# Copies of keys and queries in the token stage: one ScalarE instruction of 1280 columns, or two of 640 with a step between

## The chip, the cores and the metric

The kernel runs on one core of a Trainium2 chip. The metric is the device time of one execution in microseconds (us), as the median of several runs. Engines are called PE (TensorE, matrix products), PEld (its weight loads), DVE (VectorE), ACT (ScalarE), POOL (GpSimd) and SP (SyncE, which issues most DMAs).

## The reference

Agent attention over 4 batches of 10048 tokens with 128 channels and 49 agents, then a mixture of 16 experts (4 groups of 4) on its output, one expert per token:

```python
a2k = sm(agents, k)              # softmax over 10048 keys, 49 x 10048 per batch
agent_v = a2k @ v                # 49 x 128
q2a = sm(q, agents)              # 10048 x 49
x = (q2a @ agent_v).reshape(40192, 128)
g_idx = argmax(x @ w_group); e_idx = argmax(x[group g] @ w_expert[g])
out[token] = g_w * e_w * (relu(x @ w1[g, e]) @ w2[g, e])      # 128 -> 1024 -> 128
```

Here sm is a softmax of the scaled product, and g_w and e_w are the softmax weights of the chosen group and expert.

## The kernel before

Products run in 16-bit floats with a split: a float32 tile x is taken as an upper half xh = fp16(x) and a lower half xl = x - xh, and products are summed over the halves. So keys, queries, values and the hidden layer each need a copy to fp16, which ACT makes, and a subtraction for the lower half, which DVE or POOL makes.

The work has three stages. In the opening (to about 55 us) the first batch's keys, values and part of its queries are worked through, and its most used expert is chosen. The token stage (about 55 to 730 us) is a stream: for three batches in the order SEQ, 20 tiles of 512 tokens each, it computes the batch's main expert on every token. Each tile has 8 units. A unit is `first` (two PE products of 512 columns into a PSUM tile ph, of which there are three buffers; `evicted`: ACT writes hh = relu(ph) as fp16, DVE writes the lower half hl, and only then is ph free) and, eight units behind, `second` (three products into po). A last stage works the fourth batch, whose tokens have been sorted by expert.

Between the units of the token stage lies side work for the batches that come later in the stream: key scores, values, query scores, routing. It is written as Python generators, called lanes (`QUEUE`: q0 to q3 are queries, k1 to k3 keys and values, a0 to a3 what follows, p3 the sorting transfers). After each unit `advance` deals steps of lanes: the one that is furthest behind its due share goes first, as long as a budget of DVE and ACT time per unit (`RATE`, 900 and 1100 ns) is not used up. The time of an instruction is counted by `Counted`; for ACT it is 190 ns and 0.83 ns per column. A lane's progress is the sum of these, ACT's with weight 0.7 (`WL`), over a fixed total (`TOTALS`: 55.1e3 for a key lane, 26.2e3 for a query lane). A generator that yields an integer n isn't taken up again before n units have passed (`HOP` is 2); a bare yield lets others go on in the same unit. Where a tile of the stream needs something that isn't there, `own_tile` forces lanes on without regard to these.

`split_load` (from line 276) makes the halves of one chunk of keys or queries: 10 tiles of 128 tokens, 1280 columns (`CT * P`), the last one of a batch 1152 or 1088. It takes the loaded float32 tile xf, issues one ACT copy xh of all columns, yields HOP, and then issues POOL's subtractions for xl in pieces of 256 columns, five per full chunk. The scores of the chunk (`key_scores`, `query_scores`) come later in the lane and use xh and xl on PE: for each group of five tiles first the products with xh, then those with xl. The tiles xh and xl have three buffers each, shared with the values' halves. In the opening (`early` given, or `wide[0]` true) the same function works ahead of the stream; `wide[0]` becomes false where the token stage begins.

Each engine executes its instructions in the order of its own queue. On ACT the copies stand between the stream's evictions hh, on POOL the pieces of xl stand between the lower halves of the values (sl), of the softmax rows (rows) and sums (S). In the profile all PE, DVE and ACT instructions have line 140, that of the counting helper, so they are told apart by tile names; L304 is POOL's xl.

Of the kernel before, what the change touches and what calls it, by code (L numbers as in the profile page):

```python
# [13 lines left out]
AF = mybir.ActivationFunctionType  # L14
# [6 lines left out]
P = 128  # L21
# [34 lines left out]
HT = CT // 2  # L56
# [22 lines left out]
HOP = 2  # L79
# [68 lines left out]
def build(ctx, tc, qT, kT, v, agT, wr, w1, w2, cpk, out, cols):  # L148
# [5 lines left out]
    act = Counted(nc.scalar, work, 2, 190.0, 0.83)  # L154
# [19 lines left out]
    wide = [True]  # L174
# [17 lines left out]
    def load(kind, b, ci, xf=None):  # L192

        t0, t1 = chunks[ci]
        n = min(N, t1 * P) - t0 * P
        if xf is None:
            xf = stg.tile([P, CT * P], F32, name="xf", tag="xf")
        sync.dma_start(out=xf[:, 0:n], in_=(qT if kind == "q" else kT)[b][:, t0 * P:t0 * P + n])
        if kind == "q" and n < (t1 - t0) * P:
            vec.memset(xf[:, n:(t1 - t0) * P], 0.0)  # L200
        return xf
# [74 lines left out]
    def split_load(kind, b, ci, early=None):  # L276
        t0, t1 = chunks[ci]
        n = (t1 - t0) * P if kind == "q" else min(N, t1 * P) - t0 * P
        if (kind, b, ci) in halves:
            lane("q0")["done"] += halves.pop("work") if "work" in halves else 0.0  # L280
            yield HOP
            return halves.pop((kind, b, ci))
        xf = loaded.pop((kind, b, ci), None) if early is None else first_loads[kind, ci]
        if early is not None and kind == "k" and ci < NB:
            xh = wbuf[ci].bitcast(F16)[:, 2 * CT * P:3 * CT * P]
            xl = early.tile([P, CT * P], F16, name="xs", bufs=4)
        elif early is not None and kind == "k" and ci > len(chunks) - 3:
            xh, xl = [early.tile([P, CT * P], F16, name="xs", bufs=4) for _ in range(2)]
        else:
            if xf is None:  # L290
                xf = load(kind, b, ci)
            xh = wk.tile([P, CT * P], F16, name="xh", tag="xh")
            xl = wk.tile([P, CT * P], F16, name="xl", tag="xl")
        act.activation(xh[:, 0:n], xf[:, 0:n], AF.Copy)
        if early is None:
            yield HOP
        a = 0
        if early is not None and kind == "k":
            a = min(n, SHARED)
            vec.tensor_sub(out=xl[:, 0:a], in0=xf[:, 0:a], in1=xh[:, 0:a])  # L300
        if a < n:
            for a in range(a, n, GP):
                z = min(n, a + GP)
                pool.tensor_sub(out=xl[:, a:z], in0=xf[:, a:z], in1=xh[:, a:z])  # L304
        return xh, xl
# [49 lines left out]
    def key_load(b, ci, early=None):  # L355

        st = state[b]
        if ci == 0:
            st["S"] = rt.tile([P, NT, NA], F32, name="S", tag="S")
            st["most"] = rt.tile([P, CT, NA], F32, name="most", tag="most")  # L360
            st["part"] = []
        st["k", ci] = yield from split_load("k", b, ci, early)
        yield
# [427 lines left out]
    def query_load(b, ci, x, early):  # L791
        x["x"] = yield from split_load("q", b, ci, early)
        yield
# [549 lines left out]
    def split_ahead():  # L1343

        which = next(x for x in loaded if x[0] == "q")
        w = work.copy()
        g = split_load(*which)
        while True:
            try:
                next(g)  # L1350
            except StopIteration as x:
                halves[which] = x.value
                halves["work"] = halves.get("work", 0.0) + float(np.dot(work - w, WL))
                break
# [338 lines left out]
    def lane(name):  # L1693
        return next(y for y in lanes if y["name"] == name)
# [157 lines left out]
```

## Time and profile before

| | us |
|---|---|
| median of 3 runs | 914.24 (911.54 to 914.42) |
| profiled execution | 907.38 |
| its span, first to last instruction | 905.1 |
| PE busy in the span | 844.7 (93%) |
| DVE busy | 710.8 (79%) |
| ACT busy | 613.8 (68%) |
| POOL busy | 462.9 (51%) |
| mean granted TensorE clock | 0.982 |

Busy times are unions of instruction spans on one engine. PE is pipelined and the ends of its products are modelled, so a PE that is shown busy is not one at its peak. The profiled execution is one of many and lies below the three timed runs.

### The profile page before, as it was taken

What the parts mean: (1) busy time and instruction counts of PE and PEld (TensorE: products, weight loads), DVE (VectorE), ACT (ScalarE), POOL (GpSimd) and SP (SyncE); (2) the same over time, 40 slices, a digit from 0 to 9 for tenths busy, and PEclk for the clock granted to TensorE, in tenths of its full rate; (3) what the DMA queues carried; (4) which work ended last, traced back from release to release, by engine and by line L of the source; (5) the groups of instructions that cost most, each with busy time, mean ns of one, the idle gap of its engine ahead of it and who ended that gap; (6) DMA issues with size and microseconds to landing.
All of it is one profiled execution on the core that took longest, in us unless ns stands there. A gap on an engine that the chain in (4) does not pass through costs nothing.

```text
span 905.1 us, 22546 instructions
## 1 busy us (share of the span) xinstructions
PE 844.7 (93%) x8668; PEld 502.2 (55%) x8669; DVE 710.8 (79%) x1442; ACT 613.8 (68%) x1078; POOL 462.9 (51%) x616
## 2 busy tenths in 40 slices
PE   4889999999797999898999999999999999999995
PEld 3745455555354555454455555554444477777775
DVE  7767898886799886688989689799977666766663
ACT  6568897867486777677678787766565555555552
POOL 4387495446426451838474343646555214444454
PEclk9989999999899999999999999999999999999998
DMA  9677436453554564434536222334756445555542
GB/s 360 245 244 272 139 108 225 157 163 128 173 170 130 169 196 147 156 115 152 169 112 242 83 75 104 112 102 151 230 176 212 138 140 165 174 190 187 176 141 98
DMA packets 58578, 149.95 MB, mean 166 GB/s; under 512 B 8702, under 2 KB 19830, under 8 KB 58460
## 3 DMA queue, kind: packets, MB, share of 16 engines
q1 hardware_dynamic: 53307, 138.11, 45.4%
q0 software_dynamic: 5152, 10.30, 3.2%
q8 instruction: 70, 1.15, 0.5%
q14 instruction: 49, 0.39, 0.1%
HBM read 108.33 MB, written 38.71 MB: 162 GB/s over the span
## 4 chain that ended last, share of the span: by engine, by line
PE 41%; DVE 8%; ACT 3%; DMA 2%; issue 2%; POOL 2%; POOLq 0%; ACTq 0%; DVEq 0%
PE po L140 24%; PE ph L140 12%; PE at L140 6%; DVE hl L140 3%; POOL xl L304 1%; ACT hh L140 1%; DMA out<-oo,er 1%; DVE vl L140 1%; DMA vf<-v 1%; DVE mq L140 1%; DVE ef L140 1%; ACT vh L140 1%; DVE oo L140 0%; POOL out L1485 0%; ACT es L140 0%
## 5 line engine op out<-in xcount | busy, mean ns | idle before, releaser
L140 DVE SCALAR_TENSOR_TENSOR hl<-ph,hh 128x512 f16<-128x512 f32 (+1 forms) x562 | 374.6, 677 | 125.7 <-ACT hh L140 122.0
L140 ACT ACTIVATE hh<-ph 128x512 f16<-128x512 f32 (+1 forms) x562 | 330.0, 594 | 188.2 <-PE ph L140 110.5
L140 PEld LDWEIGHTS <-wbuf 128*128 128x128 f16 (+2 forms) x2812 | 241.2, 97 | 282.6 <-issue 50.3
L140 PE MATMUL ph<-et,wbuf 98*128 98x512 f16 (+2 forms) x1048 | 317.4, 378 | 17.7 <-DVE hl L140 17.1
L140 PE MATMUL po<-hh,wbuf 128*128 128x512 f16 (+1 forms) x960 | 287.2, 379 | 0.0
L304 POOL TENSOR_TENSOR xl<-xf,xh 128x256 f16<-128x256 f32 x278 | 183.2, 696 | 137.1 <-ACT xh L140 124.4
L140 PE MATMUL po<-hl,wbuf 128*128 128x512 f16 (+1 forms) x480 | 181.3, 378 | 0.0
L1485 POOL DMA_INDIRECT out<-oo,er x82 | 80.7, 984 | 110.7 <-ACT hh L140 53.0
L140 PE MATMUL po<-wbuf,hh 128*128 128x128 f16 x1312 | 116.6, 219 | 0.0
L1199 POOL DMA_INDIRECT sorted_rows<-rows,slot x79 | 79.0, 1000 | 67.7 <-ACT hh L140 47.1
L140 PE MATMUL po<-wbuf,hl 128*128 128x128 f16 x656 | 112.9, 219 | 0.0
L140 PEld LDWEIGHTS <-hh 128*128 128x128 f16 x1312 | 99.2, 98 | 9.0 <-issue 9.0
L140 ACT ACTIVATE xh<-xf 128x1280 f16<-128x1280 f32 (+2 forms) x58 | 72.5, 1255 | 17.2 <-PE at L140 12.2
L510 POOL TENSOR_TENSOR sl<-S,sh 128x245 f16<-128x245 f32 (+2 forms) x51 | 37.8, 764 | 53.5 <-ACT sh L140 53.5
L140 PEld LDWEIGHTS <-hl 128*128 128x128 f16 x656 | 64.2, 98 | 0.0
L847 POOL TENSOR_TENSOR rows<-ef,rows 128x245 f16<-128x245 f32 (+1 forms) x62 | 39.9, 666 | 42.8 <-ACT rows L140 42.8
L140 PEld LDWEIGHTS <-xh 128*128 128x128 f16 x1166 | 46.3, 98 | 21.6 <-issue 2.2
L140 DVE SCALAR_TENSOR_TENSOR hl<-at,hh 128x512 f16<-128x512 f32 x82 | 55.8, 680 | 0.0
L140 DVE SCALAR_TENSOR_TENSOR vl<-vf,vh 128x640 f16<-128x640 f32 (+2 forms) x51 | 48.4, 956 | 7.2 <-ACT vh L140 7.2
L140 ACT ACTIVATE et<-at 98x512 f16<-98x512 f16 (+3 forms) x81 | 47.4, 596 | 8.8 <-PE at L140 8.7
L140 ACT ACTIVATE hh<-at 128x512 f16<-128x512 f32 x82 | 49.5, 604 | 0.0
L140 DVE TENSOR_TENSOR oo<-po,oo 128x512 f32<-128x512 f32 (+1 forms) x60 | 40.3, 672 | 9.6 <-PE po L140 6.2
(330 smaller groups left out, 1042.8 us busy)
## 6 DMA issues: line engine op xcount, KB each, us to landing
wbuf<-wdr SPq DMA_DIRECT2D x22, 832.0 KB
vf<-v SPq DMA_DIRECT2D x28, 645.0 KB
xf<-qT SPq DMA_DIRECT2D x27, 640.0 KB
xf<-kT SPq DMA_DIRECT2D x25, 640.0 KB
cols<-oo SPq DMA_DIRECT2D x60, 256.0 KB
oo<-cwt SPq DMA_DIRECT2D x57, 256.0 KB
erow<-rows SPq DMA_DIRECT2D x12, 490.0 KB
er<-sorted_rows SPq DMA_DIRECT2D x19, 256.0 KB
```

The costliest lines, as they stand in the source:

```text
L140: ins = f(*a, **k)
L304: pool.tensor_sub(out=xl[:, a:z], in0=xf[:, a:z], in1=xh[:, a:z])
L510: pool.tensor_sub(out=sl[0:m, y][:, z], in0=x[:, z], in1=sh[0:m, y][:, z])
L847: pool.tensor_sub(out=x0[:, a:z, NA:2 * NA], in0=ef[:, a:z], in1=x0[:, a:z, 0:NA])
L1199: ins = pool.indirect_dma_start(out=sorted_rows[:, :], out_offset=bass.IndirectOffsetOnAxis(ap=at, axis=0), in_=x, in_offset=None, bounds_ ...
L1485: ins = pool.indirect_dma_start(out=out, out_offset=bass.IndirectOffsetOnAxis(ap=to, axis=0), in_=y, in_offset=None, bounds_check=N - 1, o ...
```

## The change

Where the token stage runs and the chunk isn't one of the opening's, the copy of xh is issued in parts of at most 640 columns (`HT * P`), with a yield of one unit behind each part and a yield of HOP - 1 behind the last. For a chunk of 1280 or 1152 or 1088 columns these are two parts, so the units that pass from the first copy to POOL's pieces are two as before. In the opening the code is what it was.

```diff
-        act.activation(xh[:, 0:n], xf[:, 0:n], AF.Copy)
-        if early is None:
-            yield HOP
+        if early is None and not wide[0]:
+            for a in range(0, n, HT * P):
+                z = min(n, a + HT * P)
+                act.activation(xh[:, a:z], xf[:, a:z], AF.Copy)
+                yield 1
+            yield HOP - 1
+        else:
+            act.activation(xh[:, 0:n], xf[:, 0:n], AF.Copy)
+            if early is None:
+                yield HOP
```

## Rows read from the trace of the kernel before

**Rows 1.** The chain that ended last: share of the span by engine
```profile
PE 41%; DVE 8%; ACT 3%; DMA 2%; issue 2%; POOL 2%; POOLq 0%; ACTq 0%; DVEq 0%
```
**Rows 2.** Busy us (instructions) by stage: PE, PEld, DVE, ACT, POOL; clock, DMA, GB/s
```profile
60.00:590.00 530.00, 498.61 (x4912) 272.10 (x4909) 439.15 (x850) 403.12 (x697) 287.96 (x429) 0.98 0.46 152
...
590.00:726.00 136.00, 135.68 (x767) 64.94 (x766) 113.79 (x284) 81.96 (x145) 66.30 (x67) 1.00 0.51 168
```
**Rows 3.** Waits of PE from 60 to 590 us: total us, times, longest
```profile
PE ph L140 <- DVE hl L140: 16.4, 11, 5.6
PE at L140 <- POOL xl L304: 6.9, 8, 2.8
```
**Rows 4.** Timeline of PE: start us, us, instruction, count [idle before <- releaser]
```profile
232.03 1.01 PE L140 MATMUL ph<-et,wbuf 98*128 98x512 f16 x2 [5.56 <-DVE hl L140]
...
383.97 0.30 PE L140 MATMUL at<-agh,xl 128*128 128x49 f16 x5 [2.81 <-POOL xl L304]
...
430.48 0.59 PE L140 MATMUL ph<-et,wbuf 98*128 98x512 f16 x2 [3.24 <-DVE hl L140]
```
**Rows 5.** Busy us by stretch, behind two stalls (clock is the third last column)
```profile
232.00:236.00 4.00, 3.97 (x10) 1.43 (x10) 3.90 (x18) 1.18 (x4) 0.00 (x0) 0.50 0.23 34
...
385.00:389.00 4.00, 4.00 (x30) 2.16 (x29) 2.60 (x4) 2.83 (x7) 3.61 (x8) 0.64 0.72 232
```
**Rows 6.** ACT's copies xh from 55 to 590 us: ns min/median/max, first and last start
```profile
L140 ACT ACTIVATE xh<-xf x52: 1109/1270/1357, 56.3 to 563.4; 128x1280 f16<-128x1280 f32 x45, 128x1152 f16<-128x1152 f32 x4, 128x1088 f16<-128x1088 f32 x3
```
**Rows 7.** ACT's groups by shape, 60 to 590 us: busy us, mean ns, idle before
```profile
L140 ACT ACTIVATE hh<-ph 128x512 f16<-128x512 f32 x346 | 203.6, 599 | 66.8 <-PE ph L140 63.9 <-DVE hl L140 0.9
L140 ACT ACTIVATE xh<-xf 128x1280 f16<-128x1280 f32 x44 | 55.9, 1273 | 16.1 <-PE at L140 11.4 <-POOL xl L304 2.4 <-DVE vl L140 1.0
...
L140 ACT ACTIVATE rows<-ef 128x490 f16<-128x490 f32 x26 | 16.4, 631 | 0.3
...
L140 ACT ACTIVATE hh<-ph 128x384 f16<-128x384 f32 x16 | 7.7, 490 | 6.8 <-PE ph L140 6.8
...
L140 ACT ACTIVATE vh<-vf 128x1024 f16<-128x1024 f32 x3 | 3.1, 1045 | 0.0
```
**Rows 8.** Timeline of ACT, DVE and PE about 431 us
```profile
430.12 1.25 ACT L140 ACTIVATE xh<-xf 128x1280 f16<-128x1280 f32 x1
431.27 0.58 ACT L140 ACTIVATE hh<-ph 128x512 f16<-128x512 f32 x1
...
431.93 0.65 DVE L140 SCALAR_TENSOR_TENSOR hl<-ph,hh 128x512 f16<-128x512 f32 x1
...
432.63 1.01 PE L140 MATMUL ph<-et,wbuf 98*128 98x512 f16 x2 [0.91 <-DVE hl L140]
```
**Rows 9.** Timeline of POOL, DVE and ACT about 224 us
```profile
218.73 12.61 POOL L304 TENSOR_TENSOR xl<-xf,xh 128x256 f16<-128x256 f32 x20
...
223.94 0.17 DVE L140 TENSOR_TENSOR coe<-at,cem 128x16 f32<-128x16 f32 x1
224.15 7.22 DVE L140 TENSOR_TENSOR coe<-coe,cog 128x16 f32<-128x16 f32 x1
...
226.51 1.27 ACT L140 ACTIVATE xh<-xf 128x1280 f16<-128x1280 f32 x1 [0.44 <-PE at L140]
233.07 0.60 ACT L140 ACTIVATE hh<-ph 128x512 f16<-128x512 f32 x1 [5.29 <-PE ph L140]
```
**Rows 10.** POOL's full xl pieces, 55 to 590 us: busy us, mean ns, idle before
```profile
L304 POOL TENSOR_TENSOR xl<-xf,xh 128x256 f16<-128x256 f32 x253 | 167.4, 698 | 131.5 <-ACT xh L140 118.8 <-PE at L140 9.8 <-DMA vf<-v 2.5
```
**Rows 11.** Timeline of POOL: three runs of xl behind idle time
```profile
57.68 8.38 POOL L304 TENSOR_TENSOR xl<-xf,xh 128x256 f16<-128x256 f32 x13 [4.00 <-ACT xh L140]
...
243.35 4.72 POOL L304 TENSOR_TENSOR xl<-xf,xh 128x256 f16<-128x256 f32 x8 [12.01 <-ACT xh L140]
...
375.70 12.26 POOL L304 TENSOR_TENSOR xl<-xf,xh 128x256 f16<-128x256 f32 x20 [4.08 <-ACT xh L140]
```
**Rows 12.** Timeline of ACT from 376 to 381 us: two evictions that follow each other
```profile
376.46 0.60 ACT L140 ACTIVATE hh<-ph 128x512 f16<-128x512 f32 x1
378.92 1.27 ACT L140 ACTIVATE xh<-xf 128x1280 f16<-128x1280 f32 x1 [1.85 <-POOL xl L304]
380.10 0.59 ACT L140 ACTIVATE hh<-ph 128x512 f16<-128x512 f32 x1
```

## The prediction

> **What bounds the kernel now.** I read the summary of engines first, then the busy time by stage, then the waits of TensorE, then the stalls one by one, and last the two engines behind them. The chain that ended last is mostly TensorE's [rows 1]. By stage, TensorE is busy 498.6 of the 530 us from 60 to 590 us, the part of the token stage that still carries side work, and 135.7 of the 136 us behind it [rows 2]. The side work that the change touches ends at 563 us, so a change of time can come only from the 31.4 us in which TensorE stands still before 590 us, and from clock lost behind such gaps. The waits name two causes: first-layer products wait for a PSUM buffer that VectorE's residual (hl) frees, 16.4 us in 11 waits, and scores wait for the lower halves (xl) that GpSimd makes, 6.9 us in 8 waits [rows 3]. Few long stalls make up much of it: 5.56, 2.81 and 3.24 us among them [rows 4]. After such a stall the granted clock is low for a while: 0.50 over four microseconds behind the first, 0.64 behind the second [rows 5], so a stall costs (1 - 0.50) x 4 = 2.0 us or (1 - 0.64) x 4 = 1.4 us more than its length. ScalarE is busy 403.1 of the 530 us [rows 2]: it has room, and matters by its order, not its sum.
>
> **The change part by part.** 52 copies of keys and queries (xh) start after 55 us [rows 6]; by the code these are the ones behind the opening, and all are split: 45 of 1280 columns into 640 + 640, seven shorter ones into 640 and a rest. TensorE's and GpSimd's instructions and all DMAs stay as they are. Two things move: ScalarE's queue gets one more instruction per chunk, with, as a rule, an eviction of the stream (hh) between the halves, and the planner counts more work.
>
> *Added ScalarE time.* No row shows a copy of 640 columns. Between 490 columns at 631 ns and 1024 at 1045 ns, 640 come to 631 + 150 x 414/534 = 747 ns; a pair takes 1.49 us where one of 1280 took 1.27 [rows 7], 0.22 us more. The next ScalarE instruction starts 0.10 us before a copy ends (430.12 + 1.25 against 431.27) [rows 8], so the queue loses some 0.12 us per pair: 52 x 0.12 = 6.2 us, and at most 52 x 0.22 = 11.4 us. Nearly all of it lies in the 127 us in which ScalarE idles. On the path are about ScalarE's share of the chain, 3% [rows 1], and more in crowded stretches; I take +0.5 us, between 0 and +11.4.
> [...]
>
> *Evictions behind a copy.* An eviction now waits for at most 0.75 us of copying instead of 1.27. Where would that have shortened a stall? The case that looks best is TensorE's 0.91 us wait at 432.63, with a copy at 430.12 ahead of the eviction. But the residual it waits for runs at 431.93, right behind the eviction (431.27 + 0.58 = 431.85) on a VectorE that shows no idle time before it [rows 8]. VectorE's queue ended that wait as well. I take 0 us, between -0.9 and 0.
>
> *The longest stall.* At 224.15 us a VectorE product of 16 columns with two SBUF inputs takes 7.22 us, its neighbour of the same size 0.17. It ends when GpSimd's unbroken run of 20 xl pieces (218.73 + 12.61 = 231.34) ends [rows 9]: it evidently can't get in while GpSimd runs piece after piece, and TensorE then lacks PSUM for 5.56 us. The last five pieces of that run belong to the copy at 226.51; it could run ahead because the next eviction (233.07) stood behind it. With the split, that eviction stands between the halves and waits for TensorE, which waits for VectorE. So the second half can't run, GpSimd gets only the two pieces that lie in the first 640 columns, runs dry, and VectorE is let in three pieces earlier. At 12.61/20 = 0.63 us from piece to piece this is 3 x 0.63 = 1.9 us. Bounds: 0, if the new order of the lanes puts no such product there, or the halves lie side by side; and -(5.56 + 2.0) = -7.6 us, if the product no longer meets a run. I take -1.9.
> By spans, a piece is 0.698 us [rows 10] and the term would be -2.1 us. [...]
>
> *Lower halves earlier.* In three runs GpSimd had idled for the copy (57.68, 243.35 and 375.70) [rows 11], and TensorE waited for xl behind each. Say the copy is issued at T. Before, three of five pieces were left at T + 1.27 + 0.08 + 2 x 0.63 = T + 2.61 us. Now these three need the second half, which comes one step of the lane later. A step is a unit of the stream: 346 + 16 evictions in 530 us [rows 7, 2], 1.46 us. So they can start at T + 1.46 + 0.75 + 0.08 = T + 2.29, 0.32 us earlier; three runs, -1.0 us. Bounds: -3 x 0.52 = -1.6 us, if the halves lie side by side; the other end is the slower rival below.
>
> *The planner.* It counts 190 + 0.83 x columns per ScalarE instruction, with weight 0.7: each split adds 0.7 x 190 = 133 to a lane's done work, 1064 in a lane of eight chunks, 1.9% of a key lane's total and 4.1% of a query lane's. So lanes are dealt later, by 2 steps for keys and up to 7 for queries, and key chunks somewhat thinner, which relieves GpSimd. I take -0.5 us (between -2.7, 0.3 us for each of three chunks in three runs, and 0). The same shift deals every chance meeting of side work anew; that is the widest uncertainty, and I size it by one stall more or fewer: 2.81 + 1.4 = 4.2 to 5.56 + 2.0 = 7.6 us [rows 4, 5].
>
> **Sum.** +0.5 + 0 - 1.9 - 1.0 - 0.5 = -2.9 us. The profiled execution took 907.38 us (a span of 905.1 and 2.28 around it) and would take 904.5. It lies 6.9 us below the median of the three runs, 914.24; I carry the difference over: 911.3 us.
>
> **The rivals.**
> *The meeting at 224 us dissolves.* With lanes dealt later and the runs of pieces broken, the two-input product meets no long run: -7.6 instead of -1.9, in sum -8.6, 905.6 us. For it: one row of 7.22 us in 439 us of VectorE work is a rare meeting. Against: the key phase still gives GpSimd five pieces per chunk.
> *Nothing to be seen.* The halves end up side by side in ScalarE's queue, or the stall is dealt back in another place: +0.5 and -0.5 remain, 914.2 us. For it: ScalarE's room, and that the evictions gain nothing.
> *Slower: the second half comes too late.* The full copy now ends nearer to its scores. The break-even of the pieces is a step of 2.61 - 0.75 - 0.08 = 1.78 us. In crowded stretches a step is longer: from the eviction at 376.46 to that at 380.10 it is 3.64 us [rows 12]. There the half that stands behind a blocked eviction delays three pieces by 3.64 - 1.78 = 1.86 us, TensorE waits in order for their scores, and its stall blocks the next eviction in turn. In the three runs this is +5.6 us and +1.4 for a drop of the clock; with +0.5 and -1.9, +5.6 in all: 919.8 us. It decides where the step between the halves is over 1.78 us. For it: those runs lie in just such stretches. Against: where GpSimd is behind by a chunk, as in the 20 pieces from 218.73, the halves are both there before it comes to them.
>
> **How the numbers follow.** The chances: forecast 0.36, the dissolved meeting 0.16, nothing 0.14, the slower rival 0.34. What a measurement of this kernel can tell from no change is about 0.3%, 2.7 us; the forecast lies just beyond it, and of its 0.36 I give 0.24 to faster and 0.12 to the same. Of the slower rival 0.04 falls within the 0.3%. Faster 0.24 + 0.16 = 0.40; same 0.12 + 0.14 + 0.04 = 0.30; slower 0.30. The forecast's own range is 908 to 914 us. The range that should hold 8 times in 10 reaches past both other cases: down to 902 (the dissolved meeting, less its neighbour's 4.2 us in part), up to 921 (the slower rival and a us more).
>
> **What the profile of the changed kernel would show.** 104 copies instead of 52, of about 0.75 us, mostly with an eviction between, and ScalarE's busy time up by 10 to 11 us; if they lie back to back, the step on the order is wrong. In the key phase no two-input VectorE instruction of several microseconds, and no run of 20 pieces; if one stands there at full length, the term of -1.9 is wrong. TensorE's waits for xl at 6 us or less; above 10 us, the slower rival holds. TensorE busy as before up to 590 us, its idle time 26 to 31 us. The forecast is wrong if the time is above 914 or below 908 us, or if it moves by stalls in which neither a copy nor a run of pieces stands.

## The result, and the profile after

The changed kernel took 921.35 us (median of 4 runs, 919.83 to 926.93), the one before 914.33 us beside it (911.54 to 914.64): 1.0106 times as long, with a 95% interval of 1.008 to 1.0132. The profiled execution took 921.58 us, its span is 919.8 us where it was 905.1, and the mean granted clock fell from 0.982 to 0.974. The forecast was 911.3 us; the time lies just above the upper end of the range (921), and on the other side of no change.

From the page of the changed kernel, the engines' line (busy time, share, instructions) and the group of the copies (busy time, mean ns, idle time before):
```profile
PE 848.7 (92%) x8668; PEld 504.4 (55%) x8669; DVE 711.3 (77%) x1442; ACT 617.1 (67%) x1130; POOL 465.0 (51%) x616
...
L140 ACT ACTIVATE xh<-xf 128x640 f16<-128x640 f32 (+1 forms) x110 | 82.1, 756 | 30.6 <-PE at L140 21.4
```
The work is the same but for 52 more ScalarE instructions (1130 against 1078 on the page before), and ScalarE's busy time grew by 3.3 us only, from 613.8. No engine has become a bound. So the loss must be idle time of TensorE and lost clock. The next fence has the windows of the changed kernel: the whole token stage with side work, then all its four-microsecond slices with a low clock (third last column; columns as in [rows 2]) but one at 0.94.
```profile
60.00:605.00 545.00, 505.94 (x4951) 276.65 (x4950) 445.26 (x866) 408.89 (x754) 292.21 (x431) 0.97 0.46 149
...
148.00:152.00 4.00, 1.81 (x19) 0.92 (x20) 2.52 (x5) 0.68 (x1) 0.00 (x0) 0.91 0.96 334
152.00:156.00 4.00, 4.00 (x23) 2.22 (x22) 2.46 (x5) 3.01 (x7) 0.00 (x0) 0.67 0.49 174
232.00:236.00 4.00, 1.57 (x4) 0.55 (x4) 3.90 (x9) 0.52 (x1) 1.16 (x2) 0.65 0.08 17
236.00:240.00 4.00, 4.00 (x38) 2.25 (x37) 3.17 (x13) 1.95 (x6) 1.24 (x2) 0.50 0.96 317
264.00:268.00 4.00, 3.56 (x20) 1.89 (x19) 3.48 (x6) 2.23 (x5) 0.00 (x0) 0.59 0.74 177
448.00:452.00 4.00, 4.00 (x31) 1.88 (x27) 2.32 (x4) 2.67 (x4) 0.00 (x0) 0.57 0.85 296
476.00:480.00 4.00, 2.37 (x28) 1.60 (x29) 3.44 (x5) 0.74 (x1) 1.06 (x3) 0.50 1.00 333
480.00:484.00 4.00, 4.00 (x27) 2.03 (x26) 2.63 (x4) 3.20 (x6) 3.71 (x7) 0.71 0.16 63
592.00:596.00 4.00, 2.06 (x16) 0.83 (x12) 1.18 (x4) 1.67 (x3) 1.24 (x2) 0.87 0.32 101
596.00:600.00 4.00, 4.00 (x14) 1.55 (x13) 4.00 (x12) 2.43 (x5) 1.83 (x3) 0.70 0.06 17
```
The same view of the kernel before, without the slice from 232 us [rows 5] and one at 0.96:
```profile
60.00:605.00 545.00, 513.29 (x5059) 280.43 (x5056) 452.93 (x885) 413.16 (x717) 295.23 (x436) 0.98 0.46 151
...
228.00:232.00 4.00, 0.00 (x0) 0.00 (x0) 4.00 (x4) 0.00 (x0) 3.34 (x6) 0.86 0.10 34
...
236.00:240.00 4.00, 4.00 (x57) 2.36 (x55) 2.45 (x5) 2.00 (x5) 0.00 (x0) 0.79 0.94 270
288.00:292.00 4.00, 3.00 (x25) 1.88 (x25) 4.00 (x8) 0.95 (x2) 0.00 (x0) 0.61 0.59 178
...
384.00:388.00 4.00, 4.00 (x29) 2.04 (x30) 2.12 (x4) 2.52 (x5) 3.95 (x7) 0.57 0.74 246
432.00:436.00 4.00, 3.37 (x23) 1.61 (x23) 3.89 (x11) 2.35 (x5) 1.37 (x3) 0.57 0.81 268
```
This gives the ledger. TensorE stands still for 545.00 - 505.94 = 39.1 us instead of 31.7, 7.4 us more. The low slices, at (1 - clock) x 4 us each and with the two left out, come to 13.6 us instead of 8.6: there are six slow places instead of four. But the clock is low in parts of the stalls too (0.50 in the last microsecond before 234.4 us), where TensorE has no work to lose time on. Counted by TensorE's busy time in each slice, the loss is 11.1 us instead of 7.3, 3.8 us more. Together that is 11.2 of the 14.7 us by which the span grew. The page agrees: with the same 8668 instructions TensorE was busy for 848.7 us, where it was 844.7 before, so 4.0 us of the 14.7 are slower work and 10.7 are idle time. Of the idle time outside the stage 0.9 us lie in the first 60 us and 2.5 us behind 605 us; these weren't followed up.

Who TensorE waited for in the changed kernel from 60 to 600 us (total us, times, longest; compare [rows 3]):
```profile
PE ph L140 <- DVE hl L140: 13.6, 11, 3.9
PE at L140 <- DVE ef L140: 4.2, 2, 2.6
PE at L140 <- DVE vl L140: 4.0, 1, 4.0
PE po L140 <- DVE oo L140: 3.3, 1, 3.3
PE at L140 <- POOL xl L311: 3.0, 6, 1.0
```
The two waits that the prediction was about fell, hl from 16.4 to 13.6 us and xl from 6.9 to 3.0. Others came up that were not among its terms: ef, vl and oo, 11.5 us. In the kernel before (60 to 605 us), oo is not among the waits, and the other two were short:
```profile
PE at L140 <- DVE vl L140: 1.5, 3, 0.6
PE at L140 <- DVE ef L140: 1.4, 2, 0.9
```
What VectorE itself waited for, from 60 to 605 us, names two of their sources. Changed kernel:
```profile
DVE xf L140 <- POOL xl L311: 7.9, 3, 4.5
DVE oo L140 <- DMA oo<-cwt: 7.9, 3, 3.4
```
Kernel before:
```profile
DVE oo L140 <- DMA oo<-cwt: 3.5, 4, 1.3
DVE xf L140 <- POOL xl L304: 2.1, 1, 2.1
```
The first is the clearing of a short chunk's tail (a MEMSET on xf), which stands in VectorE's queue until GpSimd has read that buffer, for 4.50 us at 519.01 us; the hl behind it, whose hh was done at 515.10 us, started at 519.04. The second is the load of a combine tile that landed late: the sum oo at 149.45 us had waited 3.05 us for it. In the timeline of the changed kernel (start, length, instruction, [idle before <- releaser]) the four largest stalls, two of them from these sources, look so:
```profile
149.45 0.69 DVE L140 TENSOR_TENSOR oo<-po,oo 128x512 f32<-128x512 f32 x1 [3.05 <-DMA oo<-cwt]
150.19 0.60 PE L140 MATMUL po<-hh,wbuf 128*128 128x512 f16 x2 [3.27 <-DVE oo L140]
...
224.96 8.20 POOL L311 TENSOR_TENSOR xl<-xf,xh 128x256 f16<-128x256 f32 x13
227.58 5.61 DVE L140 TENSOR_TENSOR coe<-coe,cog 128x16 f32<-128x16 f32 x1
234.43 1.01 PE L140 MATMUL ph<-et,wbuf 98*128 98x512 f16 x2 [3.90 <-DVE hl L140]
...
470.58 6.31 POOL L311 TENSOR_TENSOR xl<-xf,xh 128x256 f16<-128x256 f32 x10
472.20 5.85 DVE L140 SCALAR_TENSOR_TENSOR vl<-vf,vh 128x640 f16<-128x640 f32 x2 [0.30 <-ACT vh L140]
477.63 0.22 PE L140 MATMUL at<-sh,vl 128*128 128x49 f16 x1 [4.00 <-DVE vl L140]
...
519.01 0.11 DVE L140 MEMSET xf<- 128x64 f32 x1 [4.50 <-POOL xl L311]
520.99 0.26 PE L140 MATMUL at<-ident,rows 128*98 128x128 f16 x1 [2.55 <-DVE ef L140]
```
Only the pair at 225 to 234 us is one that the prediction priced: the same product as in [rows 9], held for 5.61 instead of 7.22 us, with TensorE's stall down from 5.56 to 3.90. The other three stand in places where the kernel before had no stall of a microsecond. The one at 477 us is of the same kind as that at 234: the vl product stands behind a run of ten GpSimd pieces.

### The profile page after: what moved, and what is told of

The parts are those of the page before. It is cut to its first block, busy times and chain, and to the rows that moved or that the text cites. A ratio compares the mean times of both kernels' runs of the same rounds, so it can differ in the third digit from the quotient of the medians.

```text
span 919.8 us, 22597 instructions
## 1 busy us (share of the span) xinstructions
PE 848.7 (92%) x8668; PEld 504.4 (55%) x8669; DVE 711.3 (77%) x1442; ACT 617.1 (67%) x1130; POOL 465.0 (51%) x616
## 4 chain that ended last, share of the span: by engine, by line
PE 56%; DVE 9%; POOL 5%; ACT 5%; issue 4%; DMA 1%; SPq 0%; POOLq 0%; DVEq 0%; ACTq 0%
PE po L140 31%; PE ph L140 17%; PE at L140 9%; DVE hl L140 3%; ACT hh L140 2%; POOL xl L311 2%; POOL S L522 1%; POOL out L1492 1%; DVE vl L140 1%; POOL sl L517 1%; ACT xh L140 1%; DVE coe L140 1%; DVE oo L140 1%; ACT vh L140 0%; DVE ef L140 0%
## 5 line engine op out<-in xcount | busy, mean ns | idle before, releaser
L311 POOL TENSOR_TENSOR xl<-xf,xh 128x256 f16<-128x256 f32 (+1 forms) x278 | 183.7, 694 | 117.5 <-ACT xh L140 116.6
L140 ACT ACTIVATE xh<-xf 128x640 f16<-128x640 f32 (+1 forms) x110 | 82.1, 756 | 30.6 <-PE at L140 21.4
```

What stands on the lines that cost most here:

```text
L140: ins = f(*a, **k)
```

## Experiments

Theory A: the split itself costs nothing or helps, and the loss is in the order that lanes and engines are dealt once the planner sees two instructions and one more step. Theory B: the halves themselves, or the step between them, delay something. A kernel's order is made twice: the planner deals the lanes' steps while the program is written, and the compiler then orders the instructions of each engine. Ratios are to the kernel before on the same chip, with 95% intervals.

The description of the change has one thing wrong. Its loop yields one unit behind each of the two parts and HOP - 1, one more, behind them. So where the planner doesn't force a lane on, at least three units pass from the first copy to the issue of GpSimd's pieces, and not two as before. In the trace the first piece of a chunk starts 3.96 us behind the start of the first copy, in the median of the 52 chunks; in the kernel before it was 1.58 behind the copy's.

**1. The parts of the change, one at a time.** Two halves issued in one step and counted as one copy (the planner's deal is that of before):
```
+    work[2] += act.fixed + act.each * n
+    for a in range(0, n, HT * P):
+        z = min(n, a + HT * P)
+        nc.scalar.activation(xh[:, a:z], xf[:, a:z], AF.Copy)
     yield HOP
```


> Two copies of 640 columns, but issued in the same step of the lane and counted by the planner as the one of before: the lanes are dealt exactly as before, only the program's final order on each engine can move. If the instruction itself costs (52 more on ScalarE, 0.1 to 0.2 us each): +3 to +7 us, 917 to 921. If the planner's count or the step between is the cause: 914 within 3. If any new order of the side work moves the time by chance: anywhere in 905 to 924, with no relation to the 52 instructions.

Measured: 1.0066 (1.0036 to 1.0095).

One whole copy, its two units taken in two steps (the change takes three, in three steps):
```
     act.activation(xh[:, 0:n], xf[:, 0:n], AF.Copy)
-    yield HOP
+    yield 1
+    yield HOP - 1
```


> One copy of 1280 columns, then a yield of one unit and a yield of HOP - 1 in place of one yield of HOP: the step alone. ScalarE's order differs from before in a few places only. The step as cause: slower by 5 us or more. All other theories: 914 within 3.

Measured: 0.9885 (0.9835 to 0.9934).

One whole copy, counted as two:
```
     act.activation(xh[:, 0:n], xf[:, 0:n], AF.Copy)
+    work[2] += act.fixed
     yield HOP
```


> One copy of 1280 columns, one yield of HOP, but the planner counts 190 ns more, as it does for two: lanes are dealt as late as in the change, with no split. The count as cause: most of the loss, 919 to 923. The split as cause: 914 within 3. New order by chance: anywhere in 905 to 924.

Measured: 1.0075 (1.0049 to 1.0102), with the same instructions as before.

The change, counted as one copy:
```
     act.activation(xh[:, a:z], xf[:, a:z], AF.Copy)
+    if a:
+        work[2] -= act.fixed
     yield 1
```


> Two copies of 640 columns with the step between, as in the change, but the planner counts them as one. The count as cause: 914 within 3. The split as cause (second half late or the extra instruction): 919 to 923, as the change. New order by chance: anywhere in 905 to 924; the stalls would then stand in other places than in the changed kernel.

Measured: 0.9904 (0.9873 to 0.9934).

What follows: the steps are not what costs. e4 has the three of the change, e2 has one more than the kernel before, and both are faster. e3 has not one instruction more than the kernel before and is slower. So far it looked as if the planner's count alone were to blame, but e1, which keeps the count and the deal, is slower too. Its deal is that of before and still its order on the engines is not: the compiler reorders on its own.

**2. Is it the count, and by which way?** The second half's fixed 190 ns enter a lane's progress and ScalarE's budget. c1 keeps them out of the progress, c2 out of the budget:
```
+        lane["done"] += ... - WL[2] * extra[0]
```


> The change, but the 190 ns that the planner counts more per chunk are taken out of the lane's progress and left in the budget per unit. Progress as the cause (lanes are taken for further than they are, so they are dealt late): 901 to 907, as the split that was counted as one. Budget as the cause: 918 to 924, as the change. Chance of the order: anywhere in 900 to 924.

Measured: 0.9942 (0.99 to 0.9983).
```
         tokens[:] -= (work - w)[1:]
+        tokens[1] += extra[0]
```


> The change, but the 190 ns more are left in the lane's progress and taken out of the budget per unit. Progress as the cause: 917 to 924, as the change. Budget as the cause: 901 to 907. Chance of the order: anywhere in 900 to 924.

Measured: 0.999 (0.9959 to 1.0021). Two more kernels change the size of what is counted for the second half, to +95 and to -95 ns:
```
+    if a:
+        work[2] -= act.fixed / 2
```


> The change, with 95 ns counted more per chunk in place of 190. Progress as a cause that grows with the lateness: between the two ends, 908 to 916. Chance of the order: anywhere in 900 to 924, outside of 908 to 916 as likely as not.

Measured: 0.9922 (0.9898 to 0.9947).
```
+    if a:
+        work[2] -= 1.5 * act.fixed
```


> The change, with 95 ns counted less per chunk than for one copy of 1280 columns. Progress as a cause that grows with the lateness: 904 or less, 895 to 904. Chance of the order: anywhere in 900 to 924, most likely slower than the 904 of the count of one.

Measured: 1.0016 (0.9988 to 1.0044).

What follows: either edit removes the loss, and from -95 over 0 and +95 to +190 ns the ratios are 1.0016, 0.9904, 0.9922 and 1.0106. No cause that grows with the count makes such a row. That spoke for chance in the deal, and called for orders that don't move.

**3. The order held.** Every engine's final order is written out and enforced by dependencies that carry no semaphore; only the copies differ, the halves standing side by side or the whole copy standing where the first half stood:
```
+    for a, b in zip(order, order[1:]):
+        tc.add_manual_dep(mine[b], mine[a].name, ...)
```
The order of before, with halves:

> Every engine's order of instructions is held to that of the kernel before; only the 52 copies are two halves side by side. If the time comes from the order: 1.000 of before, within 0.004. If 52 more instructions cost by themselves: 1.003 to 1.008.

Measured: 0.995 (0.9931 to 0.9969).

The order of e2, with halves:

> The order of the run with the step alone (0.9885 of before), held on every engine, with each copy as two halves side by side. Order: 0.9885 within 0.004. The instructions themselves: 0.992 to 0.997.

Measured: 0.9897 (0.9877 to 0.9917); the same order with whole copies is e2, 0.9885.

The changed kernel's order, with whole copies:

> The order of the changed kernel held on every engine, but the whole copy of 1280 columns stands where the first half stood and the second half is left away. Order: 1.0106 of before within 0.004, as the change. The split as the cause of the loss: 1.000 to 1.004. If the split in itself gains, as the prediction had it (2.9 us): 1.012 to 1.015.

Measured: 1.0101 (1.007 to 1.0131); the same order with halves is the changed kernel, 1.0106.

The order of e4, with whole copies:

> The order of the split that was counted as one (0.9904 of before) held on every engine, with the whole copy where the first half stood. Order: 0.9904 within 0.004. The split as a cost: 0.982 to 0.987. The split as a gain: 0.992 to 0.996.

Measured: 1.0042 (1.002 to 1.0065); the same order with halves is e4, 0.9904.

What follows: in four orders the halves are worth -0.5%, 0.1%, 0 and -1.4%. No pair shows a cost; the 0.1% is within the intervals. The changed kernel's order costs 1.0% with whole copies too. And e1 against o1, both with side-by-side halves and one deal, 1.0066 against 0.995, shows what the compiler's order alone is worth: 1.2%. No kernel holds the order of before with whole copies, so what holding an order is worth by itself wasn't measured. The 1.2% contain it. In the four pairs it stands with the halves in o1 and o2 and with the whole copies in o3 and o4, so in their mean, -0.4%, it cancels if it is the same in each. In the traces VectorE's instructions come in one order in each pair. Theory B is out. o3's waits of VectorE show the new ones of the change again, without a half in the kernel, and so do TensorE's, below them:
```profile
DVE oo L140 <- DMA oo<-cwt: 9.6, 3, 4.1
DVE xf L140 <- POOL xl L313: 8.6, 3, 5.1
...
PE at L140 <- DVE ef L140: 5.3, 3, 3.2
PE at L140 <- DVE vl L140: 4.0, 1, 4.0
PE po L140 <- DVE oo L140: 3.6, 1, 3.6
PE at L140 <- POOL xl L313: 2.7, 5, 1.0
```
In o1 TensorE's waits from 60 to 605 us are nearly those of [rows 3] but for xl, which fell to 5.0 us:
```profile
PE ph L140 <- DVE hl L140: 15.9, 12, 5.6
PE at L140 <- POOL xl L311: 5.0, 5, 2.8
```
This is the way of gain that was forecast, but it isn't steady: o3 waited 2.7 us for xl and its twin with halves, the changed kernel, 3.0; o4 not at all and e4 0.5; e2 5.5 and o2 6.4. These waits go with the units instead. In the fourteen kernels whose order comes from a deal with three units they are 0 to 4.9 us, in the six with two units 5.0 to 11.3. The ratios don't go with the units: both groups reach from about 0.99 to about 1.01.

**4. Is the changed kernel's deal an unlucky one of many?** ScalarE's budget is nudged, in the changed kernel and in e4, which leaves every instruction alone:
```
-RATE = np.array([900.0, 1100.0])
+RATE = np.array([900.0, 1090.0])
```
The changed kernel at 1090:

> The change with ScalarE's budget per unit at 1090 in place of 1100 ns in the planner. The count as the cause: 1.005 to 1.016 of before. Chance of the order: anywhere in 0.985 to 1.015.

Measured: 1.0073 (1.004 to 1.0105).

The changed kernel at 1130:

> The change with the budget at 1130 ns. The count as the cause: 1.005 to 1.016. Chance of the order: anywhere in 0.985 to 1.015.

Measured: 0.9983 (0.9953 to 1.0012).

e4, the second half not counted, at 1090:

> The split counted as one, with the budget at 1090 ns. The count as the cause: 0.985 to 0.995. Chance of the order: anywhere in 0.985 to 1.015.

Measured: 1.0022 (0.9988 to 1.0057).

e4 at 1130:

> The split counted as one, with the budget at 1130 ns. The count as the cause: 0.985 to 0.995. Chance of the order: anywhere in 0.985 to 1.015.

Measured: 0.9931 (0.9891 to 0.997).

The changed kernel at 1070:

> The change with the budget at 1070 ns. A tendency of the count: slower than its partner by 0.5% or more. Pure chance: faster than its partner as likely as slower; both anywhere in 0.985 to 1.015.

Measured: 1.0048 (1.0025 to 1.0072).

e4 at 1070:

> The split counted as one, with the budget at 1070 ns. A tendency of the count: faster than its partner by 0.5% or more. Pure chance: either way.

Measured: 1.009 (1.006 to 1.0119).

What follows: counted twice the four deals give 0.9983 to 1.0106, counted once 0.9904 to 1.009. The groups overlap, and the pairs at 1100, 1090, 1130 and 1070 differ by +2.0, +0.5, +0.5 and -0.4%. The change's 1.0106 is the slowest of its group, its twin e4 the fastest of the other. Whether counting twice shifts the middle of the deals (1.0053 against 0.9987 here) four pairs don't settle; that stays open. Nor did any run tell which step of the planner makes a deal good.

## Why the prediction was wrong

*Added ScalarE time.* Right for the copies. Those of 640 columns take 736 ns each (forecast 747), and 46 of 52 pairs have an eviction between the halves. The group of the copies is busy for 9.6 us more on the page (82.1 against 72.5). ScalarE as a whole, forecast at 10 to 11 us more, rose by 3.3 only: 52 more starts, each some 0.10 us ahead of the end before it [rows 8], would take back about 5 us, an estimate. In held orders no cost of time is to be seen.

*Evictions behind a copy.* Taken at nothing; no run isolates it, and o1 to o4 leave no room for a cost.

*The longest stall.* The size came out, by luck; the step did not. TensorE's stall shrank by 1.7 us (forecast 1.9). It was to shrink because the second half would stand behind a blocked eviction and GpSimd would run dry. But in the changed kernel no eviction held the second half back, and both halves were through long before the product ended at 233.2 us:
```profile
227.25 0.74 ACT L140 ACTIVATE xh<-xf 128x640 f16<-128x640 f32 x1 [1.15 <-PE at L140]
...
228.82 0.73 ACT L140 ACTIVATE xh<-xf 128x640 f16<-128x640 f32 x1
```
GpSimd's run went on unbroken through all pieces of that chunk. The product was held for 5.61 us because it came when nine pieces were left instead of twelve [rows 9], which is the new order's doing. The prediction's own sign, no two-input instruction of several microseconds in the key phase, failed. In o1, where the halves stand side by side, the product stayed at 7.10 us: the bound of nothing that the prediction gave for that case. And that such a product is kept out whenever it meets a run, as the prediction had it, is wrong (last section).

*Lower halves earlier.* The waits fell, but not for the reason given: those for xl are 3.9 us less in the changed kernel (1.0 was forecast), and 2.7 us in all in o3, which has its order and no halves. So the fall came with the order, and only the 1.9 us in o1 can be the halves'. The working also took two units from copy to pieces where there are three. The halves start 1.37 us apart in the median (forecast 1.46), eight pairs lie over the break-even of 1.78 us.

*The slower rival.* Its time of 919.8 us was close, its mechanism is refuted. It needed growing waits for xl, above 10 us; they are 3.0. The time went by another way to the same side. A match of the total would have passed for a confirmation, had only the total been looked at.

*The planner.* This is the step that failed. Its term was -0.5 us, and of the new deal it said that "I size it by one stall more or fewer". It reckoned with the count alone and not with the third unit. The new deal made 11.2 us in the stage: three new stalls of 2.6 to 4.0 us, with slow slices behind two of them, a slow slice behind a 2.15 us stall at 263 us and one behind many short waits at 444 us, and two microseconds more near 592 us. The long stalls of before at 289 (2.44 us), 384 and 430 us [rows 4] went in the same deal, so the new ones had to outweigh them. The prediction saw the mechanism ("deals every chance meeting of side work anew") and named as its own sign of error "stalls in which neither a copy nor a run of pieces stands"; at 149 us there is neither. But it priced one stall and gave it no sign, while over thirty waits of TensorE are dealt at once (32 of more than 0.15 us before, 35 after) and TensorE's idle time moved by 7.4 us with 3.8 us of clock behind it. In the eighteen kernels here with another order than that of before, the ratios run from 0.9885 to 1.0106; the effects that were worked out on the copies are 0.3 to 0.5% of the time. The sum of -2.9 us has the right sign and size for one order held fixed (o1: -0.5%, about -4.6 us, though its largest term, the stall at 224 us, came to nothing there) and was no forecast for the kernel that was to be built.

The two fastest versions are e2, whole copies with one more step (0.9885), and the same order with halves, o2 (0.9897). By what was just said they are lucky orders more than better ideas.

## What to carry to other kernels

Where a planner and a compiler deal the order, an edit is two edits: what it does to the instructions, and a new deal. Measure the first with the order held in both versions, and the size of the second by nudging a setting that touches no instruction; here it was 2% from end to end, some four times the edit's own effect. A forecast for a small edit in such a kernel should give the new deal its own wide, two-sided term, and the good order should be kept by writing it out.

## What the runs showed of the hardware

**A run of GpSimd lets VectorE in, or it doesn't.** The prediction took from one row that a product with two SBUF inputs can't get in while GpSimd runs piece after piece. In o3 the same product begins in such a run and takes 0.37 us (the timeline's window cuts the run):
```profile
227.43 3.82 POOL L313 TENSOR_TENSOR xl<-xf,xh 128x256 f16<-128x256 f32 x6
...
229.02 0.37 DVE L140 TENSOR_TENSOR coe<-coe,cog 128x16 f32<-128x16 f32 x1
```
The clearest pair are o4 and e4, one order. Whole copies, o4: two vl products take 7.13 us, because the first is kept out up to the end of ten pieces, at 470.80 us:
```profile
464.49 6.31 POOL L315 TENSOR_TENSOR xl<-xf,xh 128x256 f16<-128x256 f32 x10
464.82 7.13 DVE L140 SCALAR_TENSOR_TENSOR vl<-vf,vh 128x640 f16<-128x640 f32 x2
471.54 0.22 PE L140 MATMUL at<-sh,vl 128*128 128x49 f16 x1 [5.66 <-DVE vl L140]
```
Halves, e4: the same two take 2.30 us inside a run that goes on for ten microseconds:
```profile
457.80 10.42 POOL L313 TENSOR_TENSOR xl<-xf,xh 128x256 f16<-128x256 f32 x15
458.43 2.30 DVE L140 SCALAR_TENSOR_TENSOR vl<-vf,vh 128x640 f16<-128x640 f32 x2
```
Over the twenty profiles, some 230 products of these two kinds (coe with two SBUF inputs, and vl) began within an xl piece behind which at least four more GpSimd instructions followed without a gap. 23 of them ended only when the run did, held for up to 8.00 us (e3); the rest but one (2.54 us) were in after about the piece in progress: in the kernel before and the changed one these took 0.33 to 1.34 us, where a run's pieces start 0.63 us apart. The time into the piece at which they began doesn't tell which: coe entered at 0.16 and 0.33 us and was kept out at 0.11 and 0.34. What decides stays open. So part of the 1.4% between e4 and o4 is such a meeting that fell well or badly, and not the halves' merit.

**It goes with the time, and isn't the cause of this loss.** Five of the twenty kernels have no such held product: 0.9885, 0.9904, 0.9922, 0.9942 and 1.0022. The other fifteen, the kernel before among them, run from 0.9897 to 1.0106 and average 1.0025. But the two kernels of this case lose alike by it: held products of 7.22 and 3.57 us before, 5.61 and 5.38 after, with stalls of TensorE behind them of 5.56 and 2.44 us before, 3.90 and 4.00 after. In o3 the meeting of the coe product is gone and the time is that of the changed kernel, but other stalls are longer there (4.21 us at 262 us, 2.15 in the changed kernel). No run took the meeting away by itself, so what it is worth wasn't measured.

**The clock behind a stall costs half of it or more again, or nothing.** The prediction had 1.4 to 2.0 us per stall. The next windows of the changed kernel begin where TensorE goes on after the stalls of 3.27, 3.90 and 4.00 us (clock is the third last column):
```profile
150.20:156.20 6.00, 6.00 (x42) 3.21 (x43) 4.36 (x7) 3.88 (x7) 0.00 (x0) 0.72 0.65 243
234.40:240.40 6.00, 5.97 (x43) 2.96 (x43) 5.17 (x18) 2.87 (x6) 1.30 (x2) 0.53 0.76 251
477.60:483.60 6.00, 5.97 (x51) 3.44 (x52) 4.07 (x8) 3.61 (x6) 3.48 (x6) 0.61 0.56 186
```
At (1 - clock) x 6 us they lost 1.7, 2.8 and 2.3 us. The 2.55 us stall at 521 us cost no clock: the granted one was 1.00 from 521 to 527 us.
